# Scores of the later blocks as 64x64 tiles without the masked pieces, and a new order of the tasks behind the first 258

## The chip, the cores and the metric

One core of a Trainium2 chip runs the kernel. The metric is the device time of one execution in microseconds; the kernel before takes 287.81 us, the median of three runs (287.62 to 287.82).

## What is computed

Attention with a sliding window of 128 keys and a linear bias per head, then a feed-forward layer of two matrix products with a squared ReLU between them. There are 8 sequences of 576 positions with 8 heads of 64, 4608 tokens of 512 in all, and 2048 hidden units.

```
scores = scale * np.matmul(q, k.transpose(0, 1, 3, 2))
rel = pos[:, None] - pos[None, :]
mask = (rel >= 0) & (rel < 128)
scores = np.where(mask, scores + bias[None], -1000000000.0)
attn = softmax(scores)
x = (attn @ v) as (4608, 512)
r = np.maximum(x @ w_in, 0.0)
out = (r * r) @ w_out
```

A query sees its own key and the 127 before it. So for a block of 128 queries only two blocks of keys count: its own, of which the keys behind the query are masked, and the one before it, of which the keys too far back are masked.

## The kernel before

**Blocks.** A sequence has four blocks of 128 positions and a half block of 64. The blocks are numbered 0 to 39 in the order of the work. Blocks 0 to 3, 20, 21, 30 and 31 are first blocks of a sequence and have only their own keys ("diag"). Blocks 4 to 9, 12 to 17, 22 to 27 and 32 to 37 have two blocks of keys ("full"). Blocks 10, 18, 28 and 38 are pairs, the half blocks of two sequences in one ("half").

**A block of attention**, for a full block `m`, in the function `job`: the scores are matmuls with keys as the stationary operand and queries as the moving one, so that the result has the keys on the partitions and the queries in the columns. The head dimension of 64 takes half of the array's rows, and two heads (r = 0 and 1) stand in the two halves of the rows. The two halves of the work are the tasks `s{m}.0` and `s{m}.1`: each is 8 matmuls of 64 rows, 128 stationary columns and 128 moving columns (L745), into two banks of PSUM. ScalarE takes the exponential of each of the four banks, 512 columns (`e{m}.0` to `e{m}.3`, L777), into the tile `P`. VectorE multiplies `P` by a table of decayed masks that holds the bias, the window and the causal mask: `m{m}.0` for heads in the first half and `m{m}.1` for the rest, 1024 elements each (L772). The products with the values are `pv{m}.0` and `pv{m}.1` (L874), each behind its own mask; then come a reciprocal and the division (`r`, `n`; L888, L901) and a transpose into `xT` by a DMA (`x{m}`). For a pair (L851, L856) the own scores are one 128x128 piece per head, and the ones against the key blocks before are two pieces of 64 columns; the 64x64 corners of the own scores that mix the two sequences are cleared by `pmask`.

**The feed-forward layer** goes by groups of 512 tokens, 0 to 8. From group 2 on, the first product is made with one level of Strassen's method (`f{g}.{u}.{p}`, L1116): seven products, with copies of sums out of PSUM (`s1.`, `s2.`, `s5.`, L428 or L430), sums (`c11.`, `c12.`, `c22.`, L1137) and squares (`sq`, L980 on ScalarE, L982 on VectorE). The second product does the same (`p{g}.{p}.{z}`, L1271, with the sums `S1` to `S4` at L1417, copies `s1_`, `s2_`, `s3_`, `s5_` and the results `c11_`, `c12_`, `c22_` and their stores `st`). The copies and the squares may go to ScalarE or to VectorE.

**The order.** Every piece of work is a task with its tiles. A string, `ORDER`, names all 1709 tasks in order, with the engine of each (nothing for TensorE, `a` ScalarE, `d` VectorE, `g` GpSimd, `s` SyncE) and the numbers of the PSUM banks and tiles that it takes. Each engine does its own tasks in that order, and waits only for the data and the tiles.

Of the kernel before, what the change touches and what calls it, by code (L numbers as in the profile page):

```python
# [11 lines left out]
AF = mybir.ActivationFunctionType  # L12
# [66 lines left out]
squ0.2.2:d m4.1:d squ0.3.1:d m5.0:d u0.1.3::1 u0.2.3::5 pv4.0::6 m5.1:d r4.0:d n4.0:d e6.2:a e6.1:a reluu0.3.2:a:0
e6.3:a pv4.1::2 pv5.0::4 pv5.1::0 tp7.0::7 u0.0.4::6 tp7.1::3 reluu0.2.3:a:3 ev7.0.0:a reluu0.0.4:a:1 ev7.1.0:a r5.0:d  # L80
r4.1:d r5.1:d m6.0:d n5.0:d n5.1:d n4.1:d u0.3.3::7 m6.1:d xp5.0::2 xp4.0::3 pv6.0::6 reluu0.3.3:a:2 x4.0:a squ0.0.4:d
x5.0:d squ0.2.3:d pv6.1::0 r6.0:d squ0.3.2:d squ0.3.3:d S1.0.0:d s7.0::7,4 reluu0.1.3:a:1 r6.1:d e7.0:a e7.1:a m7.0:d
us0.0:d s7.1::2,5 e7.3:a e7.2:a n6.0:d m7.1:d us3.0:d n6.1:d squ0.1.3:d us0.1:d S3.0.0:d us2.0:d u1.0.2::3 u1.0.0::7
u1.0.6::4 u1.0.4::2 reluu1.0.4:a:2 squ1.0.4:a u1.0.1::6 reluu1.0.0:a:1 squ1.0.0:a xp6.0::2 pv7.1::0 r7.1:d pv7.0::5
r7.0:d n7.0:d n7.1:d u1.0.7::1 u1.0.5::7 lkq8:g lkq12:g kqT8:s kqT12:s lkq9:g kqT9:s lkq10:g xp7.0::0 x7.0:a u1.0.3::5
S2.0.0:d x6.0:d reluu1.0.7:a:1 squ1.0.7:d us1.0:d us1.1:d us3.1:d reluu1.0.1:a:2 u1.1.6::0 reluu1.0.6:a:0
reluu1.1.6:a:1 squ1.0.6:a squ1.0.1:d us2.1:d reluu1.0.2:a:3 reluu1.0.3:a:0 squ1.0.2:a u1.1.3::1 u1.1.1::4 u1.1.4::0
reluu1.1.4:a:2 pm1:d pm2:d ws0.0:d squ1.0.3:a u1.1.5::5 u1.1.2::0 squ1.1.6:a reluu1.1.2:a:1 squ1.1.2:d S1.0.1:d
reluu1.1.3:a:0 S2.0.1:d squ1.1.4:a u1.1.0::3 u1.1.7::0 reluu1.1.1:a:1 squ1.1.1:a pm0:a us3.3:d us1.3:d reluu1.1.5:a:1
reluu1.1.0:a:2 squ1.1.5:a reluu1.0.5:a:3 squ1.0.5:a p0.2.0::1 p0.2.1 p1.1.0::4 p0.1.0::6 p1.1.1 p0.1.1 us0.2:d ws1.0:d  # L90
ws0.1:d ws0.3:d S3.0.1:d p0.5.0::7 ws0.2:d us2.3:d us0.3:d ws1.1:d ws1.3:d us2.2:d S4.0.1:d S4.0.0:d p0.5.1 squ1.1.0:d
S1.1.0:d ws1.2:d s1_0:a:0 p0.6.0 p0.6.1 s1_1:a:1 squ1.1.3:a s5_0:a:2 reluu1.1.7:a:0 squ1.1.7:a c11_0:d S2.1.0:d
us3.2:d S1.1.1:d us1.2:d s8.1::0,3 s8.0::5,2 s2_0:a:3 e8.0:a e8.3:a e8.1:a e8.2:a p0.3.0 p0.3.1 s9.1::3,1 s9.0::2,5
p0.7.0 p0.7.1 e9.0:a e9.3:a e9.2:a e9.1:a lv8:g lv9:g lv10:g kqT10:s s10.0::1,2 s10.1::3,0 lkq13:g lkq15:g lkq14:g
lv12:g lkq16:g lv13:g lv14:g kqT13:s kqT15:s c12_0:d S2.1.1:d m8.1:d m8.0:d c22_0:d p1.2.0::5 p1.2.1 m9.1:d e10.0:a
e10.1:a e10.3:a e10.2:a c11_1:d S3.1.0:d m10.1:d m9.0:d s12.1::0,2 s12.0::1,7 p0.4.0 pv8.0::5 pv8.1::3 r8.0:d r8.1:d
n8.0:d m10.0:d n8.1:d e12.0:a e12.3:a e12.1:a e12.2:a kqT14:s kqT16:s p1.6.0 p0.4.1 s3_0:a:4 pv9.0::2 pv10::7,5 r9.0:d
m12.1:d n9.0:d pv9.1::0 r9.1:d n9.1:d r10.0:d m12.0:d n10.0:d p1.6.1 xp8.0::2 p1.5.0::6 pv12.1::0 pv12.0::3 xp9.0::7
s2_1:a:5 p1.5.1 x8.0:a x9.0:a S3.1.1:d r12.1:d r10.1:d r12.0:d n12.0:d n10.1:d n12.1:d S4.1.1:d S4.1.0:d s13.0::3,7
s13.1::2,1 xp10.0::5 xp12.0::0 p1.7.0 p1.7.1 e13.0:a e13.1:a s5_1:a:6 e13.3:a e13.2:a m13.0:d x12.0:d x10.0:d ut2.0:d  # L100
s15.0::0,1 s14.0::7,3 s14.1::2,5 e15.0:a e14.0:a e15.1:a e14.2:a e14.1:a e14.3:a p1.3.0 p1.3.1 m13.1:d ut2.1:d c22_1:d
f2.0.5::1 pv13.1::2 pv13.0::3 m15.0:d c12_1:d ut2.2:d r13.0:d r13.1:d m14.0:d n13.0:d m14.1:d n13.1:d lkq17:g lv15:g
lv16:g lkq18:g st0.7.2:s st0.7.3:s st0.3.1:s kqT17:s st1.7.3:s st1.7.2:s st0.3.0:s s15.1::5,6 s16.0::7,0 e16.0:a
e16.1:a s5.2.0:a:2 p1.4.0 pv14.0::3 f2.0.1::7 f2.0.2::0 pv14.1::2 s1.2.0:a:7 r14.0:d n14.0:d m16.0:d e15.3:a e15.2:a
c11.2.0:d:0 ut2.3:d r14.1:d m15.1:d f2.0.3 pv15.0::3 f2.0.6 s2.2.0:a:7 f2.1.1::6 s16.1::0,5 f2.0.7 p1.4.1 c12.2.0:d:2
e16.2:a e16.3:a c22.2.0:d:3 r15.0:d pv15.1::5 f2.1.2::1 f2.1.5::0 s1.2.1:a:7 sqc12.2.0:a s5.2.1:a:2 f2.1.6 f2.0.4
reluf2.0.4:a:2 sqc11.2.0:d n14.1:d m16.1:d n15.0:d r15.1:d c11.2.1:d:0 f2.1.3 pv16.0::3 pv16.1::1 s2.2.1:a:7
sqc11.2.1:a s17.0::7,2 e17.0:a sqc22.2.0:a lkq21:g lkq20:g lv18:g lkq22:g lv17:g n15.1:d sqf2.0.4:d r16.0:d r16.1:d
c12.2.1:d:2 n16.0:d f2.2.1::5 f2.1.7 n16.1:d c22.2.1:d:0 s1.2.2:a:7 e17.1:a f2.2.5::0 f2.2.2::3 f2.3.1::1 f2.3.2::7
c11.2.2:d:3 s1.2.3:a:2 c11.2.3:d:1 sqc22.2.1:a f2.2.6 s2.2.2:a:7 s17.1::3,2 f2.3.6 f2.1.4 f2.2.7 s5.2.2:a:2 e17.2:a  # L110
f2.2.3 f2.3.5::3 sqc12.2.1:d sqc11.2.2:d S1.2.0:d s2.2.3:a:3 c22.2.2:d:3 sqc11.2.3:d reluf2.1.4:a:2 s5.2.3:a:2 f2.3.7
c12.2.2:d:0 c22.2.3:d:1 e17.3:a sqc22.2.2:a sqc12.2.2:d m17.1:d m17.0:d p2.1.0::6 f2.2.4 f2.3.4 p2.1.1 f2.3.3 s3_1:a:2
reluf2.2.4:a:0 sqf2.2.4:d sqc22.2.3:d c12.2.3:d:0 sqc12.2.3:d S2.2.0:d sqf2.1.4:a pv17.1::5 pv17.0::4 reluf2.3.4:a:3
sqf2.3.4:a st1.2.1:s st0.2.0:s st1.3.1:s st0.2.1:s st1.2.0:s st1.3.0:s kqT18:s x14:s x13:s x15:s x16:s kqT20:s kqT21:s
kqT22:s s18.0::1,2 s18.1::0,7 p2.2.0::3 p2.2.1 S1.2.1:d S2.2.1:d r17.0:d S4.2.1:d S3.2.1:d r17.1:d n17.0:d e18.0:a
e18.1:a s1_2:a:3 S3.2.0:d n17.1:d m18.0:d p2.5.0::2 p2.6.0 p2.5.1 p2.6.1 f3.0.1::5 f3.0.2::4 f3.1.1::1 s2_2:d:7
e18.2:a e18.3:a s1.3.0:a:5 ut3.0:d ut3.1:d m18.1:d ut3.2:d c11.3.0:d:0 ut3.3:d c11_2:d f3.0.5::7 f3.0.6 s2.3.0:a:1
s5.3.0:a:0 s1.3.1:a:5 p2.7.0 f3.1.5::0 f3.0.7 s5.3.1:a:6 c22.3.0:d:3 f3.0.3 f3.1.6 s2.3.1:a:0 f3.1.3 s20.0::3,4
c12.3.0:d:1 sqc12.3.0:d c12.3.1:d:2 f3.1.7 f3.0.4 pv18::0,7 c22.3.1:d:1 sqc11.3.0:d r18.1:d S4.2.0:d r18.0:d n18.0:d
n18.1:d e20.0:a e20.1:a m20.0:d s5_2:a:0 s20.1::4,3 reluf3.0.4:a:0 e20.2:a e20.3:a m20.1:d f3.1.4 p2.7.1 f3.3.1::0  # L120
sqf3.0.4:a reluf3.1.4:a:0 s22.1::7,3 s22.0::4,5 s1.3.3:d:6 sqc12.3.1:d e22.0:a e22.3:a e22.2:a e22.1:a lv20:g lv21:g
lv22:g lkq23:g lkq24:g lkq25:g lv23:g lkq26:g kqT23:s p2.3.0 pv20.0::4 pv20.1::1 p2.3.1 r20.1:d r20.0:d n20.0:d
n20.1:d c12_2:d f3.1.2::7 c11.3.1:d:2 c22_2:d f3.2.5::4 f3.3.2::1 f3.2.1::2 pv21.0::5 pv21.1::7 r21.0:d f3.2.2::3
s5.3.2:a:1 f3.3.6 f3.2.3 s1.3.2:a:5 f3.2.6 sqf3.1.4:a r21.1:d n21.0:d n21.1:d c11.3.2:d:0 sqc11.3.1:a p2.4.0
s2.3.2:a:5 f3.2.7 f3.3.5::3 c11.3.3:d:2 m22.0:d s2.3.3:a:6 sqc22.3.0:a sqc11.3.3:a sqc22.3.1:a m22.1:d sqc11.3.2:d
c22.3.2:d:3 c12.3.2:d:2 s5.3.3:a:1 f3.3.7 pv22.0::1 p2.4.1 r22.0:d x17:s kqT24:s st2.2.1:s kqT25:s st1.4.2:s st0.4.3:s
st0.4.2:s st2.2.0:s x18:s st1.4.3:s x20:s kqT26:s x21:s sqc22.3.2:a pv22.1::7 f3.2.4 reluf3.2.4:a:3 s3_2:a:5 f3.3.3
c22.3.3:d:1 n22.0:d sqc22.3.3:d r22.1:d S1.3.0:d S2.3.0:d c12.3.3:d:1 sqc12.3.2:d f3.3.4 s23.0::2,1 s23.1::4,5
reluf3.3.4:a:0 e23.0:a sqf3.3.4:a e23.2:a e23.1:a p3.1.0::6 p3.1.1 s24.0::4,3 e24.0:a s24.1::2,0 e23.3:a e24.3:a
s1_3:a:6 sqf3.2.4:d sqc12.3.3:d n22.1:d m23.0:d S1.3.1:d S2.3.1:d p3.2.0::1 p3.2.1 s25.1::0,5 s25.0::4,7 e24.2:a  # L130
e25.0:a e24.1:a e25.3:a e25.2:a e25.1:a c11_3:d S4.3.0:d m23.1:d S4.3.1:d m24.1:d m25.0:d m24.0:d p3.6.0 pv23.0::4
# [184 lines left out]
def kernel(  # L316
# [393 lines left out]
    def job(j, kind, ms, due):  # L710
# [79 lines left out]
        if kind == "half":  # L790
            values(j, kind, 0, ms[0], nb, sP, t_P, [before[m] for m in ms], due)
            t_x[ms[1]] = t_x[ms[0]]
            return
# [687 lines left out]
```

## Time and profile before

| | |
|---|---|
| median of three runs | 287.81 us |
| the profiled execution | 288.0 us, of which its span 285.9 us |
| TensorE busy | 277.0 us, 97% |
| VectorE busy | 247.1 us, 86% |
| ScalarE busy | 207.5 us, 73% |
| GpSimd busy | 106.3 us, 37% |
| granted TensorE clock, mean | 0.997 |

The profile is of one execution. Its 288.0 us are the span and 2.1 us around it, and lie 0.2 us over the median. An engine's busy time is the union of its instructions; a matmul is shown some 0.19 us long though the next starts after 0.03 to 0.11 us, so the length of a row says less than the distance between two starts.

### The profile page before, as it was taken

What the parts mean: (1) busy time and instruction counts of PE and PEld (TensorE: products, weight loads), DVE (VectorE), ACT (ScalarE), POOL (GpSimd) and SP (SyncE); (2) the same over time, 40 slices, a digit from 0 to 9 for tenths busy, and PEclk for the clock granted to TensorE, in tenths of its full rate; (3) what the DMA queues carried; (4) which work ended last, traced back from release to release, by engine and by line L of the source; (5) the groups of instructions that cost most, each with busy time, mean ns of one, the idle gap of its engine ahead of it and who ended that gap; (6) DMA issues with size and microseconds to landing.
All of it is one profiled execution on the core that took longest, in us unless ns stands there. A gap on an engine that the chain in (4) does not pass through costs nothing.

```text
span 285.9 us, 8500 instructions
## 1 busy us (share of the span) xinstructions
PE 277.0 (97%) x3403; PEld 240.0 (84%) x3404; DVE 247.1 (86%) x566; ACT 207.5 (73%) x408; POOL 106.3 (37%) x132
## 2 busy tenths in 40 slices
PE   6799999999999999999999999999999999999994
PEld 2588999888888888898888888889889888888883
DVE  2555898799999999999999899998999979998752
ACT  4579978986588993879779958686898655657300
POOL 8977645576567026580266253430000000000000
PEclk9999999999999999999999999999999999999998
DMA  9999999999999999999999999997531220031124
GB/s 126 161 197 167 183 201 165 171 172 148 206 145 250 131 172 129 149 207 130 203 135 150 139 174 164 170 164 157 148 93 39 40 73 3 0 111 39 53 79 127
DMA packets 169062, 39.08 MB, mean 137 GB/s; under 512 B 154560, under 2 KB 169024, under 8 KB 169024
## 3 DMA queue, kind: packets, MB, share of 16 engines
q0 software_dynamic: 115184, 18.10, 87.8%
q1 hardware_dynamic: 53248, 20.00, 41.1%
q8 instruction: 26, 0.43, 0.7%
q10 hardware_dynamic: 592, 0.46, 0.6%
q14 instruction: 12, 0.10, 0.1%
HBM read 36.70 MB, written 9.44 MB: 161 GB/s over the span
## 4 chain that ended last, share of the span: by engine, by line
PE 95%; ACT 2%; DVE 1%; issue 0%; POOL 0%; DVEq 0%; POOLq 0%
PE o L1271 38%; PE h L1116 30%; PE h L1021 9%; PE s L745 6%; PE pv L874 5%; PE wm L662 2%; PE xp L921 1%; PE tp L690 1%; ACT P L823 1%; ACT rt L988 1%; PE pv L856 1%; PE o L1373 0%; PE s L805 0%; ACT masks L475 0%; PE pv L851 0%; PE s L814 0%
## 5 line engine op out<-in xcount | busy, mean ns | idle before, releaser
L1271 PEld LDWEIGHTS <-g 128*128 128x128 bf16 x704 | 67.3, 98 | 9.0
L777 ACT ACTIVATE P<-s 128x512 bf16<-128x512 f32 x120 | 64.7, 613 | 5.7 <-PE s L745 3.3
L430 ACT ACTIVATE f<-h 128x512 f32<-128x512 f32 x74 | 42.5, 601 | 25.8 <-PE h L1116 25.5
L1137 DVE CUSTOM_DVE_ANT_0 rt<-h,f 128x512 bf16<-128x512 f32 x84 | 56.4, 684 | 4.9 <-ACT f L430 1.7
L980 ACT ACTIVATE g<-rt 128x512 bf16<-128x512 bf16 x79 | 48.4, 634 | 6.4 <-DVE rt L1137 5.9
L1271 PE MATMUL o<-w_out_sb,g 128*128 128x256 bf16 x432 | 52.3, 273 | 0.0
L1116 PE MATMUL h<-xT,w_in_sb 128*128 128x256 bf16 x336 | 46.9, 273 | 0.0
L1116 PEld LDWEIGHTS <-w_in_sb 128*128 128x128 bf16 x448 | 42.2, 98 | 5.6
L616 POOL DMA_DIRECT2D kq<-in_k_dram x24 | 21.5, 895 | 57.7 <-DMA kqT<-kq 54.7
L988 ACT ACTIVATE rt<-h 128x512 bf16<-128x512 f32 (+1 forms) x61 | 35.2, 599 | 8.6 <-PE h L1116 3.9
L1271 PE MATMUL o<-wsum,sums 128*128 128x256 bf16 x288 | 35.5, 273 | 0.0
L1116 PEld LDWEIGHTS <-us 128*128 128x128 bf16 x336 | 31.9, 98 | 4.3 <-DVE ut L1085 0.2
L1271 PE MATMUL o<-wsum,g 128*128 128x256 bf16 x272 | 34.5, 273 | 0.0
L772 DVE TENSOR_TENSOR P<-P,masks 128x1024 bf16<-128x1024 bf16 x48 | 32.2, 680 | 1.3 <-ACT masks L475 0.8
L1116 PE MATMUL h<-ut,us 128*128 128x256 bf16 x224 | 31.1, 273 | 0.0
L1021 PE MATMUL h<-xT,w_in_sb 128*128 128x128 bf16 (+1 forms) x384 | 30.8, 237 | 0.1
L982 DVE TENSOR_TENSOR g<-rt 128x512 bf16<-128x512 bf16 (+1 forms) x66 | 26.1, 413 | 4.7 <-ACT rt L988 4.4
L1271 PEld LDWEIGHTS <-sums 128*128 128x128 bf16 x288 | 27.5, 98 | 3.1
L901 DVE TENSOR_TENSOR x<-pv,rec 128x256 bf16<-128x256 f32 x72 | 28.7, 417 | 0.7
L1021 PEld LDWEIGHTS <-w_in_sb 128*128 128x128 bf16 x384 | 27.0, 98 | 2.3 <-issue 0.2
L621 POOL DMA_DIRECT2D vt<-in_v_dram x28 | 25.0, 908 | 7.8 <-PE pv L856 5.3
L430 ACT ACTIVATE f<-o 128x512 f32<-128x512 f32 x29 | 17.3, 599 | 11.0 <-PE o L1271 10.0
(84 smaller groups left out, 378.1 us busy)
## 6 DMA issues: line engine op xcount, KB each, us to landing
out_dram<-f SPq DMA_DIRECT2D x62, 128.0 KB, 3.9
kq<-in_k_dram POOLq DMA_DIRECT2D x31, 128.0 KB, 6.4
kq<-in_q_dram POOLq DMA_DIRECT2D x31, 128.0 KB, 7.2
vt<-in_v_dram POOLq DMA_DIRECT2D x28, 128.0 KB, 7.5
w_out_sb<-in_moe_w_out_dram POOLq DMA_DIRECT2D x4, 512.0 KB, 11.6
w_in_sb<-in_moe_w_in_dram POOLq DMA_DIRECT2D x3, 512.0 KB, 8.6
out_dram<-f SPq DMA_DIRECT2D x15, 64.0 KB, 2.1
vf<-in_v_dram POOLq DMA_DIRECT2D x4, 128.0 KB, 4.9
```

What stands on the lines that cost most here:

```text
L430: nc.scalar.activation(o, i, AF.Copy)
L621: nc.gpsimd.dma_start(tile_of(s_v[m])[0:n, :, 0:D], source(v, m))
L772: nc.vector.tensor_tensor(flat(Pt[sP.idx], w), flat(Pt[sP.idx], w), flat(mk, w), op=ALU.mult)
L777: nc.scalar.activation(flat(Pt[sP.idx], slice(2 * i, 2 * i + 2)), sS[i].tile.rearrange("p (j t) -> p j t", j=2)[:, :, lo:hi], AF.Exp, bias ...
L901: nc.vector.tensor_tensor(o, heads(sv)[0:n, :, 0:D], sr.tile[0:n, :].unsqueeze(2).to_broadcast([n, 4, D]), op=ALU.mult)
L980: nc.scalar.activation(o, i, AF.Square, bias=0.0, scale=1.0)
L982: nc.vector.tensor_tensor(o, i, i, op=ALU.mult)
L988: nc.scalar.activation(rts[srt.idx][:, 0:n], slot.tile[:, 0:n], AF.Relu, bias=0.0, scale=1.0)
L1021: nc.tensor.matmul(slot.tile[:, f * w:(f + 1) * w], w_in_sb[:, cc, fc * 128:(fc + 1) * 128], xT[:, cc, lo % (XR * 128):lo % (XR * 128) + w ...
L1116: nc.tensor.matmul(slot.tile[:, j * 256:j * 256 + 256], a, b_, start=fresh and j == 0 and c == 0, stop=c == 1, skip_group_check=True)
L1137: nc.vector._custom_dve(TENSOR_ADD_SAT, out=rts[srt.idx], in0=slot.tile, in1=other(), s0=FMAX, s1=0.0)
L1271: nc.tensor.matmul(slot.tile[:, z * 256:z * 256 + 256], stationary(c), moving(c), start=fresh and z == 0 and c == 0, stop=c == F - 1, skip ...
```

## The change

For every full block and pair from block 8 on (20 full blocks and 4 pairs) a new function, `quarters`, makes the scores with stationary tiles of 64 rows and 64 columns: `r` picks the half of the rows (which head), `q` the half of the columns (which half of the keys), and four such tiles cover the array. The quarter of the pieces that the mask clears whole is not computed: of the block before, the first 64 keys against the last 64 queries; of the own block, the last 64 keys against the first 64 queries; in a pair, the corners that mix the two sequences. The place of the piece that is left out in the first two banks takes the own block's first corner. So `s{m}.0` now has 24 matmuls (32 in a pair) and fills two banks, and `s{m}.1` has 16 and fills half of two banks. Of the four exponentials two keep their 512 columns and two have 256. The masks still are two operations of 1024 elements, but cut by keys and not by heads: `m{m}.0` makes the own block's half of `P` for all heads (and moves the corner into place), `m{m}.1` the other half; `m{m}.0` waits for all four exponentials, `m{m}.1` for `m{m}.0`, and both `pv` tasks for both masks. The planner's costs for the new tasks do not matter to what runs, since `ORDER` sets it.

`ORDER` is written anew behind its first 258 tasks; before that only some bank numbers differ. The set of tasks is the same. The engine differs for some: 17 copies move from ScalarE to VectorE and 12 the other way, 26 squares move from ScalarE to VectorE and 28 the other way, of the evacuations `x9`, `x10`, `x12` one moves to VectorE and two to ScalarE, and of the last group's stores two move to ScalarE's queue and one to SyncE's.

```diff
-st8.4.1:s st8.4.0:s st8.3.0:a c21.1.128_8:d st8.4.1b:a
+st8.3.0:a st8.3.1:a c21.1.0_8:d st8.4.1:s c21.1.128_8:d st8.4.1b:a
...
+        if kind == "half" or kind == "full" and ms[0] >= N_PE:
+            quarters(j, ms, [at[seq[m][0], seq[m][1] - 1] for m in ms], due)
+            return
...
+    def quarters(j, ms, mbs, due):
+        m, mb, pair = ms[0], mbs[0], len(ms) == 2
+        sS = [Slot("b") for _ in range(4)]
+        t_s = []
+        def piece(z, r, i, q, col, w, mk, q0):
+            c = head_at[(i // 2) * 4 + 2 * r + i % 2] // 2
+            rows = slice(64 * r, 64 * r + 64)
+            o = i * (64 if z else 128) + col
+            nc.tensor.matmul(sS[2 * z + r].tile[64 * q:64 * q + 64, o:o + w],
+                             tile_of(s_kqT[mk])[rows, c, 64 * q:64 * q + 64],
+                             tile_of(s_kqT[m])[rows, C + c, q0:q0 + w], start=True, stop=True)
+        def scores(z):
+            for r in range(2):
+                bank(sS[2 * z + r], f"s{r}")
+            for i in range(4):
+                if z:
+                    for r in range(2):
+                        for q in range(2):
+                            piece(1, r, i, q, 0, 64, m, 64 * q if pair else 64)
+                    continue
+                for e in range(2 if pair else 0):
+                    for r in range(2):
+                        for q in range(2):
+                            piece(0, r, i, q, 64 * e, 64, mbs[e], 64 * e)
+                if pair:
+                    continue
+                for r in range(2):
+                    piece(0, r, i, 1, 0, 128, mb, 0)
+                    piece(0, r, i, 0, 0, 64, mb, 0)
+                for r in range(2):
+                    piece(0, r, i, 0, 64, 64, m, 0)
...
+            def expo(i=i):
+                P = Pt[sP.idx].rearrange("p (g r j) t q -> p r g j t q", g=2, r=2)[:, i % 2]
+                if i < 2:
+                    o, s = P[:, :, :, 0], sS[i].tile.rearrange("p (g j q) -> p g j q", g=2, j=2)
+                else:
+                    o, s = P[:, :, :, 1, 64:128], sS[i].tile[:, 0:256].rearrange("p (g j q) -> p g j q", g=2, j=2)
+                nc.scalar.activation(o, s, AF.Exp, bias=0.0, scale=scale)
...
+            elif i == 0:
+                nc.vector.tensor_tensor(P[:, :, 2:4], P[:, :, 1:4:2], units[:, :, 2:4], op=ALU.mult)
+            else:
+                nc.vector.tensor_tensor(P[:, :, 0:2], P[:, :, 0:2], units[:, :, 0:2], op=ALU.mult)
...
+            t_P.append(plan.add({"DVE": dve(1024, 2)}, due - 31 + i, lambda i=i: mask(i),
+                                t_es + (t_pm if pair else t_mask[0] + t_mask[1]) + t_P, name=f"m{m}.{i}"))
...
-                            (t_P[hf:hf + 1] if kind == "lone" else t_P[len(t_P) // 2 * hf:len(t_P) // 2 * (hf + 1)]) + [x for _, mk in parts for x in t_v[mk]],
+                            (t_P if kind == "full" and m >= N_PE else t_P[hf:hf + 1] if kind == "lone" else t_P[len(t_P) // 2 * hf:len(t_P) // 2 * (hf + 1)]) + [x for _, mk in parts for x in t_v[mk]],
```

What the orders of the engines show at three places is below. In the first, TensorE at the first half of block 8's scores; `s0`, `s1` are its banks of PSUM, `kqT_4` holds keys and queries of block 8 and `kqT_3` those of block 7. Before:

```order
L745 LDWEIGHTS kqT_3_89
L745 MATMUL s0_1314<-kqT_4_90,kqT_3_89 128x128
L745 LDWEIGHTS kqT_3_89
L745 MATMUL s1_1315<-kqT_4_90,kqT_3_89 128x128
L745 LDWEIGHTS kqT_4_90
L745 MATMUL s0_1314<-kqT_4_90 128x128
L745 LDWEIGHTS kqT_4_90
L745 MATMUL s1_1315<-kqT_4_90 128x128
```

Now, the pieces of one pair of heads:

```order
L809 LDWEIGHTS kqT_3_89
L809 MATMUL s0_1295<-kqT_4_90,kqT_3_89 64x128
L809 LDWEIGHTS kqT_3_89
L809 MATMUL s0_1295<-kqT_4_90,kqT_3_89 64x64
L809 LDWEIGHTS kqT_3_89
L809 MATMUL s1_1296<-kqT_4_90,kqT_3_89 64x128
L809 LDWEIGHTS kqT_3_89
L809 MATMUL s1_1296<-kqT_4_90,kqT_3_89 64x64
L809 LDWEIGHTS kqT_4_90
L809 MATMUL s0_1295<-kqT_4_90 64x64
L809 LDWEIGHTS kqT_4_90
L809 MATMUL s1_1296<-kqT_4_90 64x64
```

Before, a pair of heads takes four matmuls of 128 columns here, two for the block's own keys and two for those before it, with each stationary operand across all columns of the array (the sizes are keys by queries). Now it takes six, two of 128 columns and four of 64, with 64 keys each; three more pairs of heads follow in the same way, and the own block's last 64 queries go to `s8.1`.

In the second, VectorE at the masks of blocks 8 to 10, where `P` are the tiles of probabilities. Before:

```order
L772 TENSOR_TENSOR P_113<-P_113,masks 128x1024 x2
L1352 TENSOR_TENSOR f_99<-o,f_99 128x512
L772 TENSOR_TENSOR P_111<-P_111,masks 128x1024
L1341 TENSOR_TENSOR f_98<-o,f_98 128x512
L1417 TENSOR_TENSOR g_110<-g_110 128x4x256
L772 TENSOR_TENSOR P_112<-P_112,kqf 128x1024
L772 TENSOR_TENSOR P_111<-P_111,masks 128x1024
```

Now:

```order
L858 TENSOR_TENSOR P_113<-P_113,masks 128x8x128
L1134 TENSOR_TENSOR w_in_sb<-w_in_sb 128x2x256
L1429 TENSOR_TENSOR f_99<-o,f_99 128x512
L1134 TENSOR_TENSOR us_95<-w_in_sb,us_94 128x2x256
L1489 TENSOR_TENSOR sums<-sums,g_110 128x1024
L858 TENSOR_TENSOR P_111<-P_111,masks 128x8x128
L860 TENSOR_TENSOR P_111<-P_111,masks 128x8x128
L860 TENSOR_TENSOR P_113<-P_113,masks 128x8x128
```

The masks keep their number, and their sizes make the same 1024 elements. At L860 stands the second mask of a block; that of `P_111` now follows directly on the first, whose result it needs.

In the third, the end of ScalarE's queue; the DMA rows are the stores that it starts. Before:

```order
L980 ACTIVATE g_109<-rt_107 128x2x256
L1310 DMA out_dram<-f_101 128x256
L430 ACTIVATE f_99<-o 128x512
L1310 DMA out_dram<-f_100 64x256 x2
L1391 DMA out_dram<-f_102 128x128
```

Now:

```order
L430 ACTIVATE f_100<-o 128x512
L1382 DMA out_dram<-f_100 128x256
L1382 DMA out_dram<-f_103 64x256 x2
L1382 DMA out_dram<-f_103 128x256
L1463 DMA out_dram<-f_97 128x128
```

ScalarE now starts one more store of 128 rows (the last group's `st8.3.1`, which SyncE started before) between the pair of `st8.3.0` and the very last one, at L1463.

More of the change, by code (lines that the diff above doesn't have):

```diff
@@ L79 @@
[L79 to L83, printed above, removed]
@@ L99 @@
[L99 to L103, printed above, removed]
@@ L114 @@
[L114 to L118, printed above, removed]
@@ L724, in job @@
             lo, hi = (2 - nb) * 128, 256
-        else:
-            pieces = [(i * 64, 64, before[m], ms[0], i * 64) for i, m in enumerate(ms)] + [(128, 128, ms[0], ms[0], 0)]
-            lo, hi = 0, 256
         sS = [Slot("b") for _ in range(4)]
@@ L770, in mask @@
             else:
-                mk = masks if kind == "full" else pmask
-                nc.vector.tensor_tensor(flat(Pt[sP.idx], w), flat(Pt[sP.idx], w), flat(mk, w), op=ALU.mult)
+                nc.vector.tensor_tensor(flat(Pt[sP.idx], w), flat(Pt[sP.idx], w), flat(masks, w), op=ALU.mult)
         t_es = []
@@ L786, in job @@
                                 lambda i=i, nh=nh: mask(slice(nh * i, nh * i + nh)),
-                                t_es[nh // 2 * i:nh // 2 * (i + 1)] + (t_pm if kind == "half" else t_mask[1] + (t_mask[0] if kind != "diag" else [])),
+                                t_es[nh // 2 * i:nh // 2 * (i + 1)] + t_mask[1] + (t_mask[0] if kind != "diag" else []),
                                 name=f"m{ms[0]}.{i}"))
[L790 to L793, printed above, removed]
```

256 lines of the change are left out of this document (146 added, 110 removed).

## The prediction

> **What bounds the kernel now.** I read the page first: the busy times, then the chain of work that ended last.
>
> ```profile
> PE 277.0 (97%) x3403; PEld 240.0 (84%) x3404; DVE 247.1 (86%) x566; ACT 207.5 (73%) x408; POOL 106.3 (37%) x132
> PE 95%; ACT 2%; DVE 1%; issue 0%; POOL 0%; DVEq 0%; POOLq 0%
> ```
>
> TensorE (PE) is 95% of the chain. A busy PE need not be a dense PE, so next came the busy time by stretches; the first number is the stretch, then for PE, its weight loads, VectorE (DVE), ScalarE (ACT) and GpSimd the busy microseconds and the instructions.
>
> ```profile
> 46.00:282.00 236.00, 235.80 (x2783) 206.03 (x2780) 217.57 (x465) 173.78 (x330) 73.51 (x89) 1.00 1.24 130
> 60.00:220.00 160.00, 160.00 (x2073) 138.37 (x2072) 154.50 (x343) 129.06 (x248) 65.01 (x79) 1.00 1.59 155
> ```
>
> From 46 us to the end PE is never seen idle for more than 0.2 us in sum, at the full granted clock (1.00): every nanosecond taken from its stream is one off the time, if nothing else becomes late. And VectorE is second: 5.5 us of 160 are left to it while attention runs. So two questions decide: what the new scores cost TensorE, and whether VectorE still keeps ahead.
>
> **The scores on TensorE.** Here are two forms of the old scores and the products with column halves (L856) as groups, then the chain at a full block (69.73) and at a pair (103.93), then PE's timeline at L856, at a full block (from 84.66 on) and at a pair (from 103.93 on).
>
> ```profile
> L745 PE MATMUL s<-kqT 64*128 64x128 bf16 x256 | 17.2, 216 | 0.0
> L745 PE MATMUL s<-kqT,kqT 64*128 64x64 bf16 x64 | 2.3, 191 | 0.0
> L856 PE MATMUL pv<-vt,P 128*64 128x65 bf16 x64 | 1.8, 198 | 0.0
> ```
>
> ```profile
> 69.73 0.55 PE s L745 x16
> 70.28 0.98 PE o L1271 x8
> ...
> 74.74 0.87 PE o L1271 x8
> ...
> 103.93 0.56 PE s L745 x24
> ```
>
> ```profile
> 73.95 0.44 PE L856 MATMUL pv<-vt,P 128*64 128x65 bf16 x16
> ...
> 84.66 0.23 PE L745 MATMUL s<-kqT,kqf 64*128 64x128 bf16 x2
> ...
> 85.05 0.24 PE L745 MATMUL s<-kqT 64*128 64x128 bf16 x2
> 85.21 1.05 PE L1271 MATMUL o<-wsum,g 128*128 128x256 bf16 x8
> ...
> 103.93 0.22 PE L745 MATMUL s<-kqT 64*128 64x128 bf16 x2
> 103.98 0.22 PE L745 MATMUL s<-kqT,kqT 64*128 64x64 bf16 x4
> 104.04 0.22 PE L745 MATMUL s<-kqT 64*128 64x128 bf16 x2
> ...
> 104.27 0.22 PE L745 MATMUL s<-kqT 64*128 64x128 bf16 x2
> ```
>
> Seven pairs of 128 columns lie between 84.66 and 85.05: 0.056 us a pair, two matmuls at a time, one in each half of the rows. A full block streams 8 x 0.056 = 0.45 us. The change of tile shape costs extra: the next line starts 0.16 after the last pair, 0.10 of it beyond the pair; and on the way in, the chain shows the block's 16 matmuls as 0.55, so 0.10 again (the 0.98 against 0.87 of the next line is the way out). The pair of half blocks costs the same: 0.56 for its 24.
>
> The price of 64 columns has two bounds. Between 103.93 and 104.27 there are three pairs of 128 (0.168) and six pairs of 64, so 0.172 / 6 = 0.029 us a round of 64 columns with halves of the rows: the lower end. With halves of the columns, the 16 matmuls of L856 take 0.44 less the 0.198 of the last one's own length, 0.24 over seven steps: 0.035 a round, its slow first step in it: the upper end. Two at a time in both cases; four quarters at once no row shows. I take 0.032, nearer to neither, since the new tiles halve both rows and columns.
>
> If four run at once, each pair of heads needs in `s.0` two rounds (one quarter of the keys takes 128 columns, the other twice 64) and in `s.1` one: 3 x 4 = 12 rounds a block, in a pair of half blocks too. 12 x 0.032 = 0.38 against 0.45: 0.07 less, over 24 blocks **-1.6 us**. With 0.029 it is 0.10 less, -2.4; with 0.035 it is 0.03 less, -0.7.
>
> The Trainium skill speaks against it: "TensorEngine Tiling (Array Packing)", section Instruction Overhead, says that each matmul has about 60 cycles of overhead, so that one of few columns takes as long as one of 60. At the page's 2.4 GHz that would be an estimated 25 ns for each of a block's 40 matmuls, 1.0 us. The trace disagrees as far as it goes: the four short matmuls from 103.98 to 104.04 take 14 ns each. Whether it goes on so with four tiles is a rival below.
>
> The order puts the bursts of scores into 36 runs instead of 35 (counted in the two orders): one more way in and out, **+0.2**. The rest of TensorE's stream is the same set of matmuls. Startup, where PE does wait, lies before task 258 and keeps its order.
>
> **ScalarE and VectorE.**
>
> ```profile
> L777 ACT ACTIVATE P<-s 128x512 bf16<-128x512 f32 x120 | 64.7, 613 | 5.7 <-PE s L745 3.3 <-issue 1.8 <-ACT P L777 0.3
> L988 ACT ACTIVATE rt<-h 128x256 bf16<-128x256 f32 x2 | 0.8, 386 | 0.0
> L772 DVE TENSOR_TENSOR P<-P,masks 128x1024 bf16<-128x1024 bf16 x48 | 32.2, 680 | 1.3 <-ACT masks L475 0.8 <-ACT P L777 0.4
> L428 DVE COPY f<-h 128x512 f32<-128x512 f32 x10 | 6.8, 682 | 0.0
> L982 DVE TENSOR_TENSOR g<-rt 128x512 bf16<-128x512 bf16 x64 | 25.7, 417 | 3.4 <-ACT rt L988 3.1
> ```
>
> The 48 short exponentials save ScalarE 613 - 386 = 0.227 us each, 10.9 us. ScalarE is not on the chain (2%), so this is worth nothing in the time by itself. The masks have the same 1024 elements, in runs of 64 or 128: 0.68 us as now; nothing speaks for another price, but no row has runs of 64 in one operand. What VectorE gains in work comes from the engines in the order: a net five copies, one evacuation and two squares fewer. Its work overlaps at the ends, as its timeline shows:
>
> ```profile
> 103.54 0.68 DVE L1137 CUSTOM_DVE_ANT_0 rt<-h,f 128x512 bf16<-128x512 f32 x1
> 104.26 0.42 DVE L982 TENSOR_TENSOR g<-rt 128x512 bf16<-128x512 bf16 x1
> 104.60 0.69 DVE L1417 TENSOR_TENSOR sums<-sums,g 128x1024 bf16<-128x1024 bf16 x1
> 105.21 0.68 DVE L1417 TENSOR_TENSOR sums<-g 128x1024 bf16<-128x1024 bf16 x1
> ```
>
> An operation of 0.69 lets the next start after 0.61 (104.60 to 105.21), one of 0.42 after 0.34; but one that needs the result just before it starts 0.72 after it (103.54 to 104.26), 0.11 later. So 5 x 0.61 - 3 x 0.34 = +2.0 us. The second mask needs the first: in the order of VectorE it follows directly in 7 blocks, and all dependent neighbours rise from 66 to 75: 9 x 0.11 = +1.0. Together VectorE has some 3 us more to do in a stretch that is 1.6 us shorter. That comes out of the idle time, 5.5 us from 60 to 220 us and 236.0 - 217.6 = 18.4 us from 46 to 282. I count it at nothing; the cover is these idle times, and if it is gone each microsecond is one on the time (the third rival). The longer path in a block, both products with the values behind both masks and these behind all four exponentials, is covered by the other matmuls that the order puts between `s` and `pv`.
>
> The loads on GpSimd's queue and the transposes on SyncE's move with the blocks. GpSimd itself waits for free tiles, so it runs ahead of need:
>
> ```profile
> L616 POOL DMA_DIRECT2D kq<-in_k_dram x24 | 21.5, 895 | 57.7 <-DMA kqT<-kq 54.7
> ```
>
> **The end.** After the last matmuls ScalarE's queue starts three stores, and SyncE's (SPq) two:
>
> ```profile
> 280.80 1.20 ACTq L1310 DMA_DIRECT2D out_dram<-f  x2
> ...
> 281.71 1.04 SPq L1391 DMA_DIRECT2D out_dram<-f  x2
> 282.24 0.39 ACTq L1391 DMA_DIRECT2D out_dram<-f  x1
> ```
>
> The last one waits at 282.24 for its data. Now a third store stands ahead of it, which starts when the two are done (282.00) and takes between 0.39 and 0.60 (half of 1.20): the last starts at 282.4 to 282.6, 0.15 to 0.35 later than before against the matmuls' end. I take **+0.25**; SyncE's two now have one store fewer ahead of them, so they are left at nothing.
>
> **The sum.** -1.6 + 0.2 + 0.25 = -1.15 us on the profiled execution's 288.0 (its span of 285.9 and 2.1 around it): 286.85. That execution lies 0.2 over the median of the three runs, so the forecast is **286.7 us**. Its own range: -2.4 + 0.2 + 0.15 = -2.05 and -0.7 + 0.2 + 0.35 = -0.15, so 285.8 to 287.7.
>
> **The rivals.**
>
> *A quarter must end in the order in which it was issued.* In `s.0` of a full block a 64-column matmul stands right behind a 128-column one of the other half of the keys. If it may not end before it, it starts late, and the second 64 columns come only after: 0.056 + 0.032 = 0.088 in place of 0.064, and a full block takes 4 x (0.088 + 0.032) = 0.48, 0.03 more than now. 20 x 0.03 - 4 x 0.07 + 0.45 = +0.8: 288.6 us, **slower**. For it: no row of this trace has matmuls of two lengths at once. Against it: nothing but that the two halves run freely of each other in the rows shown. It decides for full blocks alone; pairs have one length. Chance 0.12.
>
> *Two at a time, whatever the tiles.* At 14 ns a matmul (from 103.98 to 104.04), 40 matmuls take 0.56, and 48 in a pair 0.67: 20 x 0.11 + 4 x 0.22 + 0.45 = +3.5: 291.3 us. For it: two is all that this trace shows. Against it: row halves and column halves both overlap, at nearly the same price. The rule cited above would be this rival's, at a higher price. Chance 0.10.
>
> *VectorE becomes the bound.* The stream gets its 1.6 us, but the new order has some product wait for a sum or a mask. Half of VectorE's extra 3 us exposed gives 286.7 + 1.5 = 288.2; with little exposed it is 287.2, with all 289.7. For it: 97% busy from 60 to 220, and more work in less time. Against it: now PE waits for nothing there, with as little room. It decides where the idle of a stretch falls under what is added. Chance 0.22.
>
> **How the numbers follow.** The forecast has 0.56. A measurement here can tell 0.2%, 0.58 us, from no change. Of the forecast's range some five sixths lie below 287.2; of VectorE's case a quarter: 0.47 + 0.05 = 0.52 faster. Between 287.2 and 288.4 are the rest of the forecast, a third of VectorE's case and a third of the first rival: 0.09 + 0.07 + 0.04 = 0.20. The rest, 0.28, is slower. The range is 285.7 to 289.3: it leaves out the second rival and the worst of the third.
>
> **What would show it.** The scores (their line then has 992 matmuls) should take 0.38 us of PE between first start and last end of a full block's two parts, with rows of four starting together; some 3980 matmuls in all; PE idle of about nothing from 46 us on. Wrong: 0.48 or 0.56 a block (first and second rival), waits of PE for `rt`, `P` or sums on VectorE (third), a last store on ScalarE's queue no later than now against the last matmul (the end), or masks unlike 0.68 us.

## The result, and the profile after

The changed kernel takes 289.81 us, the median of four runs (289.57 to 290.30), against 287.81 before: 2.0 us slower, a ratio of 1.0069 with an interval of 1.0051 to 1.0088. The forecast was 286.7, its range ended at 289.3. The profiled execution took 290.3 us, with a span of 288.1. The times of the runs below are medians of all their executions; a ratio, which leaves out four single executions that took over 1.5% longer than the fastest of their run, is not the quotient of two medians.

From the page of the profile after, the busy times, the chain's shares and the queue that brings TensorE its instructions (packets, MB, share); the last line is that queue on the page of before.

```profile
PE 276.4 (96%) x3979; PEld 240.1 (83%) x3980; DVE 249.8 (87%) x568; ACT 198.0 (69%) x406; POOL 106.2 (37%) x132
...
q8 instruction: 31, 0.51, 0.7%
...
PE 89%; POOL 3%; DMA 2%; ACT 2%; DVE 2%; issue 0%; POOLq 0%
```

```profile
q8 instruction: 26, 0.43, 0.7%
```

The stretches of after (busy us of PE, its weight loads, DVE, ACT, POOL, then the granted clock, the times of all DMA packets added up as a share of the engines' time, which can exceed 1, and GB/s):

```profile
46.00:284.00 238.00, 235.37 (x3360) 206.45 (x3358) 219.91 (x468) 164.28 (x328) 73.17 (x89) 1.00 1.31 129
60.00:220.00 160.00, 157.45 (x2602) 136.80 (x2601) 150.83 (x333) 120.48 (x248) 64.09 (x78) 1.00 1.69 157
```

TensorE, never seen idle for more than 0.2 us in sum before, is idle for 2.63 us now, 2.55 of it between 60 and 220 us. VectorE is idle for 9.2 us of the 160, where it had 5.5: it isn't what has become full.

The tiles did what was forecast. The chain at block 8, and TensorE's timeline there, where a row stands for matmuls that overlap:

```profile
61.74 0.50 PE s L809 x32
62.24 1.85 PE o L1343 x16
```

```profile
61.82 0.23 PE L809 MATMUL s<-kqT,kqT 64*64 64x64 bf16 x4
61.85 0.20 PE L809 MATMUL s<-kqT 64*64 64x64 bf16 x2
61.88 0.22 PE L809 MATMUL s<-kqT,kqT 64*64 64x128 bf16 x4
61.91 0.20 PE L809 MATMUL s<-kqT 64*64 64x64 bf16 x2
61.94 0.22 PE L809 MATMUL s<-kqT,kqT 64*64 64x128 bf16 x4
```

Six matmuls, a pair of heads, come every 0.06 us: two rounds of 0.03, with 128 columns beside 64. The block takes 0.50 on the chain where it took 0.55.

Now the loss. TensorE's timeline at the two longest of its idle times, in brackets how long and what ended it by the profile:

```profile
83.58 0.60 PE L1188 MATMUL h<-xT,w_in_sb 128*128 128x256 bf16 x4
84.85 0.61 PE L1188 MATMUL h<-ut,us 128*128 128x256 bf16 x4 [0.67 <-ACT P L847]
...
89.61 0.60 PE L1188 MATMUL h<-xT,w_in_sb 128*128 128x256 bf16 x4
91.87 0.61 PE L1188 MATMUL h<-xT,w_in_sb 128*128 128x256 bf16 x4 [1.66 <-DVE P L860]
```

Between two starts of matmuls there lie 0.94 and 1.93 us where 0.11 is usual, so 0.83 and 1.82 us are lost. The brackets look like the third rival: products behind an exponential and a mask. But follow what these two products need. The second (`f2.1.1`) takes a bank of PSUM that the division of block 13 gives back (`n13.1`, L973). VectorE's timeline:

```profile
88.96 0.41 DVE L973 TENSOR_TENSOR x<-pv,rec 128x256 bf16<-128x256 f32 x1
89.92 1.29 DVE L1209 CUSTOM_DVE_ANT_0 rt<-h,f 128x512 bf16<-128x512 f32 x2 [0.54 <-ACT P L847]
91.12 0.68 DVE L860 TENSOR_TENSOR P<-P,masks 128x1024 bf16<-128x1024 bf16 x1
```

The division ends at 89.37, half a microsecond before TensorE starts the last matmul ahead of the gap (89.94). The mask that the bracket names was the last thing to end; the product doesn't read it. The first product (`f2.0.5`) is alike: its operands are there at 83.18, its bank at 83.75, and it starts at 84.85. Nothing is missing.

What the two have in common is their number. Counted in the order of TensorE's instructions, weight loads and waits included, the first starts with instruction 2499, the second with 2755: 256 further. A third, short loss (0.40 us at 107.81, inside the scores of block 17) stands ahead of 3267, twice 256 further. And the transfers on the queue `q8` bring 16,384 bytes each: 256 instructions of 64 bytes. TensorE had run out of instructions. I call what one such transfer brings a chunk; the expectations below say page. The 576 matmuls more, with their weight loads, fill four and a half chunks, and five more are brought: 31 instead of 26.

The Trainium skill has this in "Runtime: NRT & Kernel Launch", section Instruction fetch mechanics: an engine's sequencer brings its instructions by a DMA queue of its own, in blocks of 16 KiB, 256 instructions, while it works on those before, and the cost is "mostly hidden". The trace agrees on the block; in it, 3.05 us were not hidden.

From the trace's records of that queue and the starts of the instructions, for the chunk ahead of each loss (its first instruction's start; after what time the transfer of the next one began; how long that took; what was lost). "Runs for" is the chunk's own length where nothing is lost, from the run with lighter loads below.

| chunk begins at | runs for | changed: start, delay, transfer, lost | lighter loads |
|---|---|---|---|
| 2243 | 5.39 | 78.52, 4.01, 0.97, 0.83 | 80.49, 2.09, 0.96, 0 |
| 2499 | 5.19 | 84.85, 4.74, 0.97, 1.82 | 85.88, 1.36, 0.95, 0 |
| 3011 | 7.20 | 100.19, 4.38, 1.77, 0.40 | 99.49, 1.65, 1.16, 0 |

Where TensorE waits, its first instruction comes 1.30 to 1.47 us after the transfer's end. 4.74 + 0.97 + 1.30 makes 7.0 us, and the chunk is run through in 5.2. In the kernel before, chunks between 58 and 155 us last 8.15 us and more, and the transfers begin at most 3.9 us into them: never late.

### The profile page after: what moved, and what is told of

Its sections match the earlier page's. It is cut to its first block, busy times and chain, and to the rows that moved or that the text cites. A ratio compares the mean times of both kernels' runs of the same rounds, so it can differ in the third digit from the quotient of the medians.

```text
span 288.1 us, 9635 instructions
## 1 busy us (share of the span) xinstructions
PE 276.4 (96%) x3979; PEld 240.1 (83%) x3980; DVE 249.8 (87%) x568; ACT 198.0 (69%) x406; POOL 106.2 (37%) x132
## 4 chain that ended last, share of the span: by engine, by line
PE 89%; POOL 3%; DMA 2%; ACT 2%; DVE 2%; issue 0%; POOLq 0%
PE o L1343 38%; PE h L1188 30%; PE h L1093 9%; PE pv L946 5%; PE s L809 4%; DMA w_in_sb<-in_moe_w_in_dram 2%; POOL kq L610 2%; PE s L745 1%; POOL vf L621 1%; ACT P L847 1%; PE tp L690 1%; PE o L1445 1%; PE xp L993 1%; ACT rt L1060 1%; PE pv L928 1%; DVE P L860 0%
## 5 line engine op out<-in xcount | busy, mean ns | idle before, releaser
L430 ACT ACTIVATE f<-h 128x512 f32<-128x512 f32 x70 | 40.2, 599 | 22.9 <-PE h L1188 22.1
L1343 PE MATMUL o<-w_out_sb,g 128*128 128x256 bf16 x432 | 53.3, 273 | 0.0
L847 ACT ACTIVATE P<-s 128x512 bf16<-128x512 f32 (+1 forms) x96 | 41.8, 498 | 9.7 <-PE s L809 5.9
L973 DVE TENSOR_TENSOR x<-pv,rec 128x256 bf16<-128x256 f32 x72 | 28.8, 416 | 0.7
L1054 DVE TENSOR_TENSOR g<-rt 128x512 bf16<-128x512 bf16 (+1 forms) x64 | 25.5, 412 | 3.1 <-ACT rt L1060 2.6
L430 ACT ACTIVATE f<-o 128x512 f32<-128x512 f32 x28 | 16.6, 595 | 11.2 <-PE o L1343 10.8
L616 POOL DMA_DIRECT2D kq<-in_q_dram x24 | 21.5, 895 | 1.6 <-PE h L1093 1.6
```

The lines of the kernel that those rows point to most:

```text
L430: nc.scalar.activation(o, i, AF.Copy)
L616: nc.gpsimd.dma_start(view(kq[s_kq[m].idx], i), source(src, m, split))
L847: nc.scalar.activation(o, s, AF.Exp, bias=0.0, scale=scale)
L973: nc.vector.tensor_tensor(o, heads(sv)[0:n, :, 0:D], sr.tile[0:n, :].unsqueeze(2).to_broadcast([n, 4, D]), op=ALU.mult)
L1054: nc.vector.tensor_tensor(o, i, i, op=ALU.mult)
L1343: nc.tensor.matmul(slot.tile[:, z * 256:z * 256 + 256], stationary(c), moving(c), start=fresh and z == 0 and c == 0, stop=c == F - 1, skip ...
```

## Experiments

First theory: TensorE runs out of instructions, since chunks full of short matmuls go by faster than the next one comes through the busy DMA engines. Second theory, the prediction's third rival in a milder form: the new order lets some products wait for VectorE or ScalarE. Each run is compared with the kernel before on the same chip. All spans of profiled executions are also compared from instruction 1475 on (58.08 us in both kernels), because the time that the startup takes differs by up to 2.4 us between executions: from there the kernel before takes 227.8, the changed one 230.0.

**The new order with the old tiles.**

```diff
+QUARTERED = ()
...
-        if kind == "half" or kind == "full" and ms[0] >= N_PE:
+        if kind in ("half", "full") and ms[0] in QUARTERED:
```

> The new order with the old scores (128 stationary columns, four exponentials of 512, masks by heads) in all blocks. First theory, TensorE runs out of instructions: the two long gaps of the changed kernel (0.83 us from 84.0 and 1.82 us from 90.0) and a short one at 107.8 lie 256 instructions of TensorE apart or a multiple of it, and no data is missing there; with 1152 instructions fewer they go: 289.8 - 2.9 for the gaps + 1.2 to 1.6 for the lost gain of the tiles gives 288.1 to 288.5. Second theory, the new order puts the first products of group 2 behind VectorE's and ScalarE's work: the gaps stay where they are, 290.5 to 291.5.

292.92 us against 288.1, ratio 1.0157 (1.0101 to 1.0214); 231.5 from instruction 1475 on. The losses at the chunks' ends are gone, as the first theory has it, but the time is 4 us worse than it said. Its bursts of scores take 2.0 us more than those of the run with lighter loads; seven gaps of 0.22 to 0.35 us between 139 and 217 us, none of them at a chunk's start, hold 1.9 (one lies in a burst). So the new order fits the new tiles only, and this run doesn't separate the two. That the expectation took the order for free was a miss.

**The old order with more instructions.** The same columns, cut into more matmuls, those of a full block in the first line, those of a pair in the second:

```diff
+                                cuts = [64, 64] if g2 else [48, 40, 40]
...
+                                cuts = [64] * (w // 64) if g2 else [32] * (w // 32)
+                            for i, n in enumerate(cuts):
```

> The kernel before, its order and its work on VectorE and ScalarE unchanged, but each score matmul from block 8 on cut by its moving columns, so that a block has 40 matmuls (48 in a pair) as in the changed kernel; the same columns are streamed. First theory (instructions run out): gaps of TensorE without missing data come up between 60 and 150 us, each ahead of an instruction whose number is 256 or a multiple of it behind the gaps' numbers in the changed kernel; 1 to 3 us in all, so 289 to 291, with up to 0.5 of it for the shorter matmuls themselves. Second theory (order): no gaps, 287.8 to 288.4.

292.17 us, ratio 1.0116 (1.0059 to 1.0173). Its waits of TensorE from 40 us on are one line (us in total, times, longest), and the timeline shows it inside the scores of a pair:

```profile
PE s L752 <- issue: 1.1, 1, 1.1
```

```profile
155.87 0.17 PE L752 MATMUL s<-kqT 64*128 64x32 bf16 x1
157.14 0.26 PE L752 MATMUL s<-kqT 64*128 64x32 bf16 x7 [1.10 <-issue]
```

The row at 157.14 begins with instruction 4803, 9 x 256 behind 2499: a dry chunk, in the order of before, though it is the only one and lies behind the stretch that was named. The rest of the 3.6 us that this run has over the kernel before from 1475 on is the matmuls: two at a time, a full block takes 0.64 instead of 0.55 and all bursts together 2.4 more, which I had put at up to 0.5. The starts in its trace show why: a pair of matmuls with 64 columns starts 0.029 us after the pair before it, and one with 32, 40 or 48 columns 0.025 us, so that cutting below 64 columns saves next to nothing.

**The changed kernel with lighter loads.**

```diff
+LIGHT = 13
...
-                    nc.gpsimd.dma_start(view(kq[s_kq[m].idx], i), source(src, m, split))
+                    w = 32 if m >= LIGHT else n
+                    nc.gpsimd.dma_start(view(kq[s_kq[m].idx], i)[0:w], source(src, m, split)[0:w])
...
+            w = 32 if m >= LIGHT + 4 else n
```

> The changed kernel, but the loads of keys and queries from block 13 on and of values from block 17 on bring 32 of their 128 rows; the other rows keep what an earlier block left, so that part of the input is left out. TensorE, VectorE and ScalarE have the same instructions in the same order. First theory (instructions run out, because the transfers that bring them stand behind the loads): the transfers start sooner and the gaps shrink to under 0.5 us in all, 286.9 to 287.5. Second theory (order): nothing that the products wait for is changed, 289.5 to 290.3.

287.7 us against 288.1, ratio 0.9991 (0.9966 to 1.0016); no wait of TensorE from 40 us on. Its stretches, the last two numbers being the DMA engines' share and GB/s, and the same stretch of the changed kernel:

```profile
60.00:150.00 90.00, 89.99 (x1521) 78.54 (x1520) 86.40 (x195) 69.80 (x145) 35.16 (x57) 1.00 1.08 127
```

```profile
60.00:150.00 90.00, 87.45 (x1493) 75.68 (x1492) 83.50 (x188) 67.82 (x140) 45.09 (x55) 1.00 1.96 167
```

With a share of 1.08 instead of 1.96 the transfers begin after 1.4 to 2.1 us (table above), and the three losses are gone: 226.95 from 1475 on against 230.0, 3.05 less. VectorE and ScalarE have the same work in the same order. The second theory falls here, if lighter loads help in no other way. The same loads in the kernel before test that:

> The kernel before with the same lighter loads as the third kernel (keys and queries from block 13 on and values from block 17 on bring 32 of their 128 rows; part of the input is left out). It shows what lighter loads give where no page runs dry. First theory (instructions run out): nothing, within 0.3 us of the kernel before, so that the third kernel's gain is its gaps. If lighter loads help in another way too (stores, transposes, waits): over 0.5 us less.

227.8 from 1475 on, as with full loads: TensorE gains nothing by them where no chunk runs dry. The median, 288.79 against 287.89 (1.0037, 1.0013 to 1.0061), is 0.9 over what was expected; 0.36 of it is a longer startup in the profiled execution, the rest I can't place.

**The changed kernel again, and shifted by 64 instructions.** The first is the same program on another chip, the second has 32 tiny matmuls more behind the warm-up.

```diff
+        for _ in range(32):
+            nc.tensor.matmul(s_warm.tile[:, 0:8], warm[:, 0:128], warm[:, 0:8], start=True, stop=True)
```

> The changed kernel as it is, on the same chip as the three others. First theory (instructions run out): gaps again ahead of the same products, since the pages begin at the same instructions, but not of the same length, since they hang on the traffic of the transfers: 1 to 4 us in all. Second theory (order): the same 0.83 and 1.82 us within 0.1.

> The changed kernel with 32 more matmuls of 8 columns (64 instructions with their weight loads) right behind the warm-up. Nothing else moves. First theory (instructions run out): the places where TensorE can run dry lie 64 instructions earlier in the order than before, inside the scores of block 14 and at the first of block 16, and 256 and 512 later; no gap is left ahead of the products at which the changed kernel had them. Gaps of 0 to 3 us in all, since a page of 256 now holds other work; 287 to 290.5. Second theory (order): the same two products of group 2 still wait 0.8 and 1.8 us, 289.8.

Again: 289.85 us against 288.22 (1.0040, 1.0008 to 1.0071). The waits of the one and then of the other, and the longest one of the second in its timeline:

```profile
PE s L809 <- issue: 0.6, 1, 0.6
```

```profile
PE s L811 <- issue: 2.3, 2, 1.9
PE o L1345 <- ACT f L430: 0.8, 1, 0.8
```

```profile
89.72 0.32 PE L811 MATMUL s<-kqT 64*64 64x64 bf16 x16
91.96 0.25 PE L811 MATMUL s<-kqT,kqT 64*64 64x128 bf16 x4 [1.92 <-issue]
```

In the same program, the two products of group 2 now start without a gap, and 0.82 us are lost at instruction 3267 alone; 227.8 from 1475 on is the 226.95 of the run with lighter loads and this loss. A wait for data would have come back. The first theory had expected losses ahead of all the same products, 1 to 4 us in all; which chunks run dry turned out to change from execution to execution. Shifted (291.85 us, 1.0126, 1.0077 to 1.0176, over the 287 to 290.5 of the first theory), 0.97, 2.1 and 0.56 us are lost at 1987, 2755 and 4291 of the new count, and 1.7 more at a lower clock (last section). The loss at 2755 lies inside the scores of block 16, 64 instructions earlier in the work, as said. That the places keep their distance of 256 while the work under them changes shows the mechanism. So does a time that stays: in all 14 dry chunks in the traces of this case, the runs below included, the first instruction comes 1.29 to 1.75 us after the transfer's end, whatever work it belongs to.

**Fewer instructions.** Old tiles in blocks 13 to 18; old tiles in 14, 16 and 18; and halves of all 128 columns where the mask clears nothing (`s{m}.1` of full blocks).

```diff
+QUARTERED = tuple(m for m in range(8, 40) if not 12 < m < 19)      # or: not in (14, 16, 18)
```

```diff
+                if z and not pair:
...
+                        nc.tensor.matmul(sS[2 + r].tile[:, 64 * i:64 * i + 64], tile_of(s_kqT[m])[rows, c, :],
+                                         tile_of(s_kqT[m])[rows, C + c, 64:128], start=True, stop=True)
```

> The changed kernel with the old scores in blocks 13 to 18 (five full blocks and one pair), the stretch in which the gaps lie; quarters in the other 18. First theory (instructions run out): some 280 instructions of TensorE fewer between 75 and 120 us, no gaps, and 6 blocks lose 0.07 us each: 289.8 - 2.9 + 0.4 = 287.3, faster than both kernels by a little. Second theory (order): the gaps stay, 290.2.

> The changed kernel with the old scores in blocks 14, 16 and 18 alone, so that no 256 instructions of TensorE between 78 and 108 us hold more than two blocks of quarters; quarters in the other 21. First theory (instructions run out): without gaps the changed kernel takes 0.9 us less than the kernel before; three blocks give back 0.07 each and a little in small waits, so 0.5 us under the kernel before, with gaps of up to 0.5 in some executions: 287.3 to 288.0 where the kernel before has 287.8. Second theory (order): the gaps ahead of the products of group 2 remain, 2 us over the kernel before.

> The changed kernel, but the second half of a full block's scores, in which the mask clears no piece, with tiles of 64 rows and all 128 columns: 8 matmuls of 64 columns instead of 16, so 160 matmuls and 320 instructions fewer. First theory (instructions run out): a page of 256 lasts some 10% longer where the scores stand; gaps under 1 us in all, 287 to 288.5. The tiles alone would take 4 x 0.029 instead of 4 x 0.032, no difference, unless the step from quarters to halves costs the 0.10 us of other changes of shape: then +0.1 for each of some 18 blocks whose halves stand together, +1.8. Second theory (order): 289.8.

289.65 us (1.0037, 1.0000 to 1.0074), 290.77 (1.0083, 1.0055 to 1.0112) and 290.01 (1.0070, 1.0039 to 1.0101): all slower than before, the first at the edge of what can be told from no change, where the first two were expected to be a little faster. The profiled execution of the first has no gap, 228.0 from 1475 on: its six old blocks and small waits cost 1.0 over the run with lighter loads, not 0.4. In the second the dry chunk is elsewhere, at instruction 5827, 13 x 256 behind 2499, and lost 1.3 us:

```profile
196.38 0.81 PE L1197 MATMUL h<-xT,w_in_sb 128*128 128x256 bf16 x6 [1.14 <-issue]
```

I had thinned out the chunks that ran dry in one execution, and another ran dry in the next. The second also waits twice at no chunk's start: 0.28 us at 85.48 for ScalarE and 0.75 us at 152.35, where scores wait until the transpose of a block lands; so part of its loss is the order's. The one with whole columns has no gaps either, and 228.6 from 1475 on: 1.7 over the run with lighter loads, as its expectation said for the case that a change of tile shape inside a block costs 0.10. The parts of block 8 on its chain, halves first, make 0.60 where the quarters make 0.50.

```profile
61.55 0.22 PE s L821 x8
61.77 0.38 PE s L809 x16
```

**Quarters in the old order.**

```diff
+QUARTERED = (8, 9, 10, 12, 13, 14, 17, 22, 23, 24, 25, 32, 34, 37)    # ORDER as before, masks' names exchanged
```

> The order of before with quarters in the 14 blocks in which it allows them (8 to 10, 12 to 14, 17, 22 to 25, 32, 34, 37; where the two masks stood the other way round, their names are exchanged), the old scores elsewhere. First theory (instructions run out): 0.05 us less in each of 14 blocks, so 287.1 against 287.8, if no page runs dry; the pages from 60 to 90 us are those at risk, up to 2 us. Second theory (order): no waits in this order, 287.1.

291.24 us (1.0115, 1.0066 to 1.0163), over the 287.1 to 289.1 of the first theory and the 287.1 of the second. Its waits of TensorE:

```profile
PE s L818 <- DVE sums L1498: 1.2, 1, 1.2
PE s L749 <- DVE xT L429: 0.9, 1, 0.9
PE s L818 <- issue: 0.5, 1, 0.5
PE pv L955 <- DVE P L869: 0.3, 1, 0.3
```

The first and the third are at instructions 4035 and 1987: dry chunks again, in the order of before; they lost 1.44 and 0.69 us between starts. The second and the fourth (at 82.4 and 87.9 us, 0.99 and 0.50 us) are at no chunk's start: here the old order does let TensorE wait, once ahead of scores and once for a mask.

**The end.**

```diff
-st8.3.0:a st8.3.1:a c21.1.0_8:d st8.4.1:s c21.1.128_8:d st8.4.1b:a
+st8.3.1:s ... st8.3.0:a c21.1.0_8:d st8.4.1:s c21.1.128_8:d st8.4.1b:a
```

> The changed kernel with the last group's store st8.3.1 back on SyncE's queue, ahead of the two others there; all else as changed. In the changed kernel the last store starts 1.15 us behind the last matmul's start, in the kernel before 0.66. If the third store ahead of it on ScalarE's queue is the reason: 0.7 again, 0.4 to 0.5 us less in all, part of it outside the span (2.24 us lie around the span in the changed kernel, 1.9 in the kernel before). The gaps of TensorE stay as random as they are (0 to 3 us). If the stores on SyncE's queue end last now: no gain.

> The third kernel (lighter loads, part of the input left out) with the end of the one above: what tiles and order are worth where no page runs dry and the end costs nothing. First theory (instructions run out): no gaps, 0.9 to 1.3 us less than the kernel before, 286.5 to 287.0. If something else in the new order costs time: 287.5 or more.

The ends of ScalarE's queue in the changed kernel and with the store moved back; the last matmul starts at 283.70 and 284.97:

```profile
282.92 1.83 ACTq L1382 DMA_DIRECT2D out_dram<-f  x3
284.85 0.40 ACTq L1463 DMA_DIRECT2D out_dram<-f  x1
```

```profile
285.54 0.49 ACTq L1463 DMA_DIRECT2D out_dram<-f  x1
```

The last store starts 0.57 behind the last matmul instead of 1.15, and the span ends 3.95 behind it instead of 4.38: 0.43 us, as expected, inside the span. What lies around the span stayed at 2.2, so that part of the expectation was wrong. The time, 290.48 us (1.0069, 1.0045 to 1.0092), is no better; its profiled execution (291.13 us) lost 4.1 us at instructions 2499, 2755 and 3267.

With lighter loads too, and so without dry chunks: 287.25 us against 288.28, ratio 0.9962 (0.9937 to 0.9987), 1.0 us faster. That is what tiles and order are worth, in a kernel that leaves out part of the input; a complete kernel that has it, I didn't find.

## Why the prediction was wrong, step by step

*The stream of TensorE: mechanism right, size 0.4 us too large.* Four quarters run at once, and the first two rivals are out. A round takes 0.031 us, as assumed, but the way in and out of a full block 0.12 instead of 0.10: it went from 0.553 to 0.501 between its first start and that of the next work, 0.05 and not 0.07. All bursts from instruction 1475 on, the extra run of them included, went from 14.64 to 13.64 us with lighter loads: -1.0, forecast -1.4. The estimated 25 ns for each of 40 matmuls, which the prediction set beside its own price, did not come: a block takes 0.50 us, not 1.0. But "The trace disagrees" went too far. In one and the same half of the rows, matmuls of 32, 40 and 48 columns all start 0.025 us apart (second experiment), so short matmuls do have a least price there; tiles side by side pay it at the same time, which is why the block doesn't show it. The 2.4 GHz of that estimate do not stand on the page of the Trainium skill that the prediction names.

*ScalarE and VectorE at nothing: right.* The masks in the groups of after:

```profile
L858 DVE TENSOR_TENSOR P<-P,masks 128x1024 bf16<-128x1024 bf16 x20 | 13.6, 680 | 0.0
L860 DVE TENSOR_TENSOR P<-P,masks 128x1024 bf16<-128x1024 bf16 x20 | 13.5, 682 | 0.2
```

They take 0.68 us as forecast, and with lighter loads, with all of VectorE's work and waits between the engines, TensorE is dense. The third rival, which had 0.22, looked right on the wait lines and was not it.

*The end: right in kind.* +0.25 was the forecast; the last store came +0.49 later against the last matmul's start, +0.43 of the time by the run with the store moved back, though the span's own end moved by only 0.11 between the two kernels.

*The step that failed* is "every nanosecond taken from its stream is one off the time, if nothing else becomes late", with "The rest of TensorE's stream is the same set of matmuls". The prediction counted 3980 matmuls instead of 3404 and priced them in time alone. It never asked where 1152 more instructions come from and how fast. From 58.08 us on, which is the same time in both profiled executions, the spans differ by 2.2 us: -1.05 for the bursts without the waiting in one of them, +3.05 for the three dry chunks, +0.11 for the other matmuls and +0.11 behind the last of them. The page of before would have allowed the question: 26 transfers for 285.9 us of a program with 3403 matmuls, one for about 128 of them, on DMA engines that are busy throughout attention. The sentence of the Trainium skill on the fetch ("Runtime: NRT & Kernel Launch", Instruction fetch mechanics) would have led there as well, though its "mostly hidden" speaks against looking; the 3.05 us here are the measured answer.

*What stays open.* Why the transfer of a chunk begins 4.0 and 4.7 us late for the chunks from 2243 and 2499 on in one execution, and 2.6 and 2.9 in another of the same program: the lighter loads show that the traffic matters, not which of it.

## What to carry to other kernels

When a change replaces few long instructions by many short ones, price the count as well as the time: look up how many instructions one fetch brings, find the shortest time in which the new code runs through that many, and compare it with the time from asking to having (7 us here with the DMA engines full, an estimated 4 with lighter loads: 1.4 to 2.1 until the transfer, 1.0 for it and the 1.3 behind it). When a wait line names an engine, check that the instruction needs what that engine did; a gap without missing data that comes back every 256 instructions is the fetch. And look at the same program twice: here the waits put down to ScalarE and VectorE did not come back, and the dry chunks moved.

## What the hardware showed unexpectedly

After the gap of 2.1 us in the shifted run the granted clock fell to 0.61, seen in its stretches:

```profile
92.00:96.00 4.00, 4.00 (x44) 3.04 (x45) 1.98 (x3) 2.45 (x6) 3.20 (x4) 0.61 2.13 201
```

Sixteen matmuls of 256 columns in a row started 0.104 us further apart than usual, 1.7 us once more. The gap of 1.82 us in the changed kernel had no such sequel (clock 1.00 from 60 to 220), nor had one of 2.1 us, as long as this one, in the run with the store moved back (1.00 from 92 to 96). So the length of the gap alone doesn't decide it; what does, these runs don't show.

Quarters of the array run with different numbers of columns side by side: 128 beside twice 64 in 0.06 us. A step from halves to quarters inside a block cost the same 0.10 us as one from whole tiles (0.60 us for block 8 with halves first, 0.50 with quarters alone).
